# A delta-rule attention with two feed-forward layers on one core: k loaded by tokens and turned on TensorE, v scaled before the triangular solve, weights issued earlier, weight conversion dealt out in pairs

## The chip, the cores and the metric

One core of a Trainium2 chip runs the whole program. The metric is device time in microseconds (us) of one launch, the median of repeated runs. PE is TensorE, DVE is VectorE, ACT is ScalarE, POOL is GpSimd, SP is SyncE; SP, ACT and POOL can also issue DMA transfers, each from a queue of its own, in order.

## The reference, cut to what matters

```
# attention: B=4, H=8, S=768, D=48
k_n = k / (norm(k) + 1e-6); state = zeros(B, H, D, D)
for t in range(S):
    y[:, :, t] = q[:, :, t] @ state
    v_old = state^T k_n[:, :, t]
    state += beta[:, :, t] * outer(k_n[:, :, t], v[:, :, t] - v_old)
# first layer: 3072 tokens, 384 -> 2048 -> 384
x = (s * relu(y @ w_in)**2 + b) @ w_out
# second layer: 8 experts, 384 -> 1024 -> 384, the best expert of each token by cosine / tau
out = gate * (relu(x @ w1[e]) @ w2[e])
```

## The kernel before

The sequence of 768 tokens is cut into chunks of C = 32 tokens, and four chunks (HG = 4, 128 tokens) make a group; there are NG = 6 groups. For each group the kernel prepares and then runs the attention.

- Preparation: `load_k`, `load_q`, `load_v`, `load_beta` issue the loads. k lies in `kpad` with 32 tokens by four pairs of heads on the partitions, one slot per chunk s. `tr_k` and `tr_q` turn k and q on PE into `kqt` (features on partitions), `gram` (for group 0 `gram_first`) multiplies k with k and with q, `lanes_in` transposes the products on DVE into `A` and normalises, and a triangular solve follows on DVE: `solve`, or for groups 0 and 1 `solve_d` on the two halves of the triangle, 15 steps of two instructions, after which `off_in` transposes twice (`tt`, `dd`) and `off_1`, `off_2` put the missing quarter together with 64 small matmuls each per chunk. `scale_v`, inside `lanes_in`, multiplies v by the norms of k on POOL.
- Attention of a group, `dstep` for s = 0 to 3, each three hops: `ks` (PE: state times k and q; DVE: `X`), `tx` (PE: `u`; DVE: `bdu`), then `ku` (PE: `ds`; DVE: the state `sst`) and `mu` (PE: the output into `ch`; ACT copies it to `x`). Each waits for the one before. `ku` reads k in the layout with 32 tokens by four pairs (`kpad`).

The first layer (`moe1`) runs on PE in ticks between the hops: `mm1` and `mm2` over eight pairs of weight blocks for each of 12 tiles of 256 tokens. Its products are fp32r with operands split into a high and a low part, so the weights are first converted: they lie interleaved in 16 units, and `convert()` takes each apart with two ACT operations (`w_scale`), two DVE operations, one POOL addition (L577), one ACT copy and one subtraction (L562, on POOL, or on DVE for every second unit from the sixth on). `w_step()` advances `convert()` by half a unit.

PE, DVE, ACT and POOL run in the order in which the code is written; SP's loads stand in the order in which the tile framework places them. For group 0 nothing of the first layer can run, since it needs the attention's output. For group 0 the items of the list in `attention` are keyed by hop; those with keys of 100 and more, the preparation of group 1, come after group 0's attention, with ticks of the first layer between them (`PREP`: 2 ticks after each turn, 12 after `lanes_in`, 3 after each solve step, 10 after `off_in`, 1 after each `off_`). From group 1 on, the preparation of the next group runs between the hops of this one, and `run_moe` is dealt out so that the first layer stays one group behind.

```
elif st["gi"] == 0:
    if nh % 4 == 1:
        w_step()              # one half unit per hop of group 0's attention
...
if state["n"] % 4 == 0:
    w_step()                  # and one per four ticks of the first layer
```

Of the kernel before, what the change touches and what calls it, by code (L numbers as in the profile page):

```python
# [19 lines left out]
def tile_kernel(ctx, tc, q, k, v, beta, w_in, w_out, s_in, b_in, emb, tau, w1, w2, out):  # L20
# [103 lines left out]

    def load_v(gi, eng, heads=range(B)):
# [8 lines left out]

    def load_q(gi, engines):
        i = 0
        for h in range(B):
            for g in range(2):
                engines[i % len(engines)].dma_start(
                    out=qpad[:, h, :, 64 * g:64 * g + D],  # L140
                    in_=q[h, g::2, gi * HG * C:(gi + 1) * HG * C, :].rearrange("r t d -> t r d"))
                i += 1
# [22 lines left out]
    def tr_q(gi, h, alt=False):  # L165
        pp = ps_pp.tile([128, 4, HG, C], F32, tag="pp", name="pp")
        for r in range(4):
            nc.tensor.transpose(out=pp[0:DP, r].rearrange("p n t -> p (n t)"), in_=qpad[:, h, r, 0:DP], identity=ident)
        for s in range(HG):
            o = kqt_t[gi, s][:, h].rearrange("p (a x t) -> p a x t", a=2, x=4)[:, :, 1:3, :]  # L170
            i = pp[0:DP, :, s, :].rearrange("p (a x) t -> p a x t", a=2)
            nc.scalar.copy(out=o, in_=i)
# [49 lines left out]
    ln = {}  # L222

    def lanes_in(gi):
        if gi < 2:
            Af = stg.tile([128, C + 1, C], F32, tag="A", name="A")
            Tf = stg.tile([128, C + 1, C], F32, tag="gc", name="T")
# [6 lines left out]
        nc.gpsimd.memset(Tf, 0.0)  # L234
# [27 lines left out]
        if gi > 1:  # L262
            scale_v()
        return scale_v
# [33 lines left out]
    def tail_solve(gi, scale_v):  # L298
        scale_v()
        off_in(gi)  # L300

# [8 lines left out]
    def off_1(gi, n0, n1):  # L310
# [8 lines left out]
        zz = stg.tile([128, 2 * B, n1 - n0, C2], F32, tag="tmp", name="zz")  # L319
# [109 lines left out]
    def dstep(gi, s, more):  # L429
# [6 lines left out]
        if nb:  # L436
            X = ks(gi, s, ch)
            if gi == 0:
                warm(3)
            yield  # L440
        bdu = tx(gi, s, X)
        if gi == 0:
            warm(0 if s == 0 else 2 if s == 1 else 3)
# [9 lines left out]
    def attention(more, first):  # L453
        for gi in range(NG):
# [5 lines left out]
            if gi == 0:  # L460
                add(0, first)
                for n0, n1, h in ((1, 2, 0.0), (2, 4, 2.0)):
                    add(h, off_1, 0, n0, n1)
                    add(h + 1.0, off_2, 0, n0, n1)
            if gi + 1 < NG:
                g2 = gi + 1
                sy = [nc.sync]
                if gi:
                    add(0, load_k, g2, sy)
                    add(0, load_q, g2, sy)  # L470
                    add(0, load_beta, g2)
                    add(0, load_v, g2, nc.sync)
                h = 3.25 if gi else 100
                dh = 0.25 if gi else 1
                for f in (tr_k, tr_q, gram):
                    for s in range(0, HG, 2 if f is gram else 1):
                        if gi == 1 and f is tr_k and s == 3:
                            h = max(h, 6.25)
                        add(h, f, g2, s)
                        h += dh  # L480
# [8 lines left out]
                else:  # L489
                    add(103.5, router_setup_a2)  # L490
                    add(104.5, router_setup_b)
                    lv = []
                    add(200, lambda: lv.append(lanes_in(1)))
                    for j in range(C2 - 1):
                        add(300 + j, solve_d, 1, j)
                    add(400, lambda: tail_solve(1, lv[0]))
# [19 lines left out]
            while items:  # L516
                t = items[0][0]
                due(t)
                yield PREP.get(t // 100, 2)
# [36 lines left out]
    def w_parts(n):  # L556
# [4 lines left out]
        eng = nc.gpsimd if n % 2 or n < 5 else nc.vector  # L561
        eng.tensor_tensor(out=w[:, :, 1], in0=x, in1=w[:, :, 0].bitcast(F32), op=ALU.subtract)  # L562
# [20 lines left out]
    def w_step():  # L583
        next(cg_, None)

# [212 lines left out]
    with tc.manual_schedule(engines={ET.PE, ET.DVE, ET.Activation, ET.Pool}):  # L798
        hw, sy = [nc.sync, nc.scalar], [nc.sync]
        setup()  # L800
        sq0 = stg.tile([128, 1], F32, tag="ss", name="sq0")
        nc.vector.memset(sq0, 1.0)
        nc.scalar.activation(out=sq0, in_=sq0, func=AF.Sqrt)
        load_k(0, hw)
        warm_t.append(ps_h.tile([128, 2, 256], F32, tag="h", name="warm"))
        load_beta(0, nc.gpsimd)
        w_load(W_ORDER[0])
        load_v(0, nc.sync, (0,))
        load_q(0, sy)
        for i in range(1, B):  # L810
# [398 lines left out]
```

## Time and profile before

| | |
|---|---|
| median of three runs | 1013.82 us (1010.84 to 1013.82) |
| the profiled execution | 1013.74 us, span 1011.7 us |
| mean granted PE clock | 0.914 |
| PE busy, matmul instructions | 876.2 us (87%), 13070 |
| DVE, ACT, POOL busy | 468.4, 321.8, 287.0 us |

```
PE   2587963996599799979997999999998999999997
DVE  1744698135942794269525962225314323321111
POOL 4124666113032333243323332334530110110100
PEclk9657876797599899999999999999998999999999
GB/s 111 221 56 278 34 29 66 5 34 27 49 25 34 3 50 32 49 3 45 37 18 3 18 2 18 2 17 128 46 17 49 42 38 41 47 50 162 16 32 24
```

Each digit is the busy share of a fortieth of the span (25.3 us) in tenths; PEclk is the granted clock in tenths of 2.4 GHz; GB/s is what the DMA engines moved. The first eleven digits of PE are the start, group 0, the preparation of group 1 and group 1; the rest is the first layer with groups 2 to 5, and from about 760 us the second layer.

### The profile page before, as it was taken

What the parts mean: (1) busy time and instruction counts of PE and PEld (TensorE: products, weight loads), DVE (VectorE), ACT (ScalarE), POOL (GpSimd) and SP (SyncE); (2) the same over time, 40 slices, a digit from 0 to 9 for tenths busy, and PEclk for the clock granted to TensorE, in tenths of its full rate; (3) what the DMA queues carried; (4) which work ended last, traced back from release to release, by engine and by line L of the source; (5) the groups of instructions that cost most, each with busy time, mean ns of one, the idle gap of its engine ahead of it and who ended that gap; (6) DMA issues with size and microseconds to landing.
All of it is one profiled execution on the core that took longest, in us unless ns stands there. A gap on an engine that the chain in (4) does not pass through costs nothing. (4 is left out here: it accounts for less than half of the span.)

```text
span 1011.7 us, 29675 instructions
## 1 busy us (share of the span) xinstructions
PE 876.2 (87%) x13070; PEld 803.7 (79%) x13070; DVE 468.4 (46%) x975; ACT 321.8 (32%) x674; POOL 287.0 (28%) x289
## 2 busy tenths in 40 slices
PE   2587963996599799979997999999998999999997
PEld 2374863885499799979897989999996779779896
DVE  1744698135942794269525962225314323321111
ACT  1235643142134233413341333335422222222221
POOL 4124666113032333243323332334530110110100
PEclk9657876797599899999999999999998999999999
DMA  5738213011211021202200000004103811114000
GB/s 111 221 56 278 34 29 66 5 34 27 49 25 34 3 50 32 49 3 45 37 18 3 18 2 18 2 17 128 46 17 49 42 38 41 47 50 162 16 32 24
DMA packets 115986, 49.55 MB, mean 49 GB/s; under 512 B 90328, under 2 KB 112529, under 8 KB 115857
## 3 DMA queue, kind: packets, MB, share of 16 engines
q1 hardware_dynamic: 112976, 47.23, 20.4%
q8 instruction: 103, 1.69, 0.7%
q10 hardware_dynamic: 2304, 0.39, 0.3%
q14 instruction: 27, 0.21, 0.1%
q0 software_dynamic: 576, 0.02, 0.0%
HBM read 38.06 MB, written 9.74 MB: 47 GB/s over the span
## 5 line engine op out<-in xcount | busy, mean ns | idle before, releaser
L641 PE MATMUL h<-xhl,wp 128*128 128x256 f32 x1728 | 254.0, 297 | 44.0 <-ACT r L649 30.2
L641 PEld LDWEIGHTS h<-xhl,wp 128*128 128x128 f32 x1728 | 226.1, 200 | 50.7 <-ACT r L649 33.0
L650 POOL TENSOR_TENSOR r<-r 128x512 f32<-128x512 f32 x96 | 104.6, 1090 | 352.9 <-ACT r L649 352.7
L673 PE MATMUL acc<-gh,wp 128*128 128x256 f32 x1152 | 161.5, 286 | 0.0
L673 PEld LDWEIGHTS acc<-gh,wp 128*128 128x128 f32 x1152 | 146.3, 193 | 4.4 <-issue 2.6
L653 DVE TENSOR_TENSOR gl<-r,gh 128x512 fp32r<-128x512 f32 x96 | 73.8, 769 | 129.7 <-ACT gh L652 129.5
L652 ACT CAST gh<-r 128x512 fp32r<-128x512 f32 x96 | 59.8, 622 | 149.6 <-POOL r L651 149.2
L919 DVE SCALAR_TENSOR_TENSOR hl<-h,hh 128x512 fp32r<-128x512 f32 x46 | 31.7, 691 | 141.2 <-ACT hh L918 141.2
L649 ACT ACTIVATE r<-h 128x512 f32<-128x512 f32 x96 | 57.4, 598 | 109.9 <-PE h L641 89.4
L651 POOL TENSOR_SCALAR r<-r,s_sb,b_sb 128x512 f32<-128x512 f32 x96 | 82.2, 856 | 10.0
L673 PE MATMUL acc<-gl,wp 128*128 128x256 f32 x576 | 83.9, 281 | 0.0
L673 PEld LDWEIGHTS acc<-gl,wp 128*128 128x128 f32 x576 | 74.4, 191 | 0.2
L416 ACT COPY x<-ch 32x384 f32<-32x384 f32 x96 | 45.1, 470 | 73.5 <-PE ch L402 72.5
L988 POOL TENSOR_TENSOR x2l<-xr,x2h 128x512 fp32r<-128x512 f32 x15 | 18.7, 1276 | 166.2 <-ACT x2h L987 166.2
L999 PE MATMUL o<-w2h,hh 128*128 128x384 f32 x184 | 62.3, 339 | 0.0
L999 PE MATMUL o<-w2l,hh 128*128 128x384 f32 x184 | 61.9, 336 | 0.0
L999 PE MATMUL o<-w2h,hl 128*128 128x384 f32 x184 | 61.8, 336 | 0.0
L273 DVE TENSOR_TENSOR T<-T,tmp 128x31 f32<-128x31 f32 (+15 forms) x124 | 55.2, 445 | 4.3
L916 PE MATMUL h<-x2l,w1h 128*128 128x512 f32 x120 | 51.8, 431 | 4.6 <-POOL x2l L988 4.6
L916 PE MATMUL h<-x2h,w1h 128*128 128x512 f32 x120 | 50.4, 420 | 6.1 <-ACT x2h L987 4.9
L270 DVE TENSOR_TENSOR tmp<-A,T 128x31 f32<-128x31 f32 (+15 forms) x124 | 53.5, 431 | 3.0
L918 ACT ACTIVATE hh<-h 128x512 fp32r<-128x512 f32 x46 | 27.4, 598 | 85.4 <-PE h L916 85.4
(207 smaller groups left out, 1227.6 us busy)
## 6 DMA issues: line engine op xcount, KB each, us to landing
wr<-in_moe_w_in SPq DMA_DIRECT2D x16, 384.0 KB
wr<-in_moe_w_out SPq DMA_DIRECT2D x8, 768.0 KB
v<-in_v SPq DMA_DIRECT2D x192, 24.0 KB
qpad<-in_q SPq DMA_DIRECT2D x48, 96.0 KB
x2d<-x2s SPq DMA_DIRECT2D x24, 192.0 KB
out<-o SPq DMA_DIRECT2D x24, 192.0 KB
kpad<-in_k SPq DMA_DIRECT2D x176, 24.0 KB
xr<-x2d SPq DMA_DIRECT2D x5, 768.0 KB
```

The costliest lines, as they stand in the source:

```text
L270: nc.vector.tensor_tensor(out=tmp, in0=A[:, j + 1:, j:j + 1].to_broadcast([128, m, j + 1]), in1=T[:, j:j + 1, 0:j + 1].to_broadcast([128, ...
L273: nc.vector.tensor_tensor(out=T[:, j + 1:, 0:j + 1], in0=T[:, j + 1:, 0:j + 1], in1=tmp, op=ALU.subtract)
L416: nc.scalar.copy(out=x_t[gi][pb:pb + C, :, r * 96:(r + 1) * 96].rearrange("p h (g e) -> p h g e", g=2), in_=y[32 * rr:32 * rr + 32, :, :, ...
L641: nc.tensor.matmul(out=h[:, f, :], lhsT=wi_(w, 2 * j + f, m), rhs=x[:, m, :], start=(m == 0 and i == 0), stop=(m == KD - 1 and i == 2))
L649: nc.scalar.activation(out=r, in_=h, func=AF.Relu)
L650: nc.gpsimd.tensor_tensor(out=t, in0=r, in1=r, op=ALU.mult)
L651: nc.gpsimd.tensor_scalar(out=t, in0=t, scalar1=s_sb, scalar2=b_sb, op0=ALU.mult, op1=ALU.add)
L652: later.append((step[0] + 7, lambda: nc.scalar.copy(out=gh, in_=t)))
L653: later.append((step[0] + 9, lambda: nc.vector.tensor_tensor(out=gl, in0=t, in1=gh.bitcast(F32), op=ALU.subtract)))
L673: nc.tensor.matmul(out=acc[:, m * TT:(m + 1) * TT], lhsT=wo_(w, 2 * j + f, m * 128, 128), rhs=x[:, f, :], start=(j == 0 and m not in seen ...
L916: nc.tensor.matmul(out=ps, lhsT=w[:, m, f * 128:(f + 1) * 128], rhs=x[:, m, :], start=(m == 0 and i == 0), stop=(m == KD - 1 and i == 2))
L999: nc.tensor.matmul(out=ps, lhsT=h[:, sl], rhs=w[:, f, :], start=(f == 0 and i == 0), stop=(f == KF2 - 1 and i == 2))
```

## The change

- k of groups 0 and 1, and every q, come with `load_n`: 128 tokens on the partitions, one transfer for a head pair's four rows, 8 transfers for a group in place of 32. Group 0's k is split over SP's and ACT's queues, its q stands on ACT's queue. `tr_n` turns k and q alike. The other layout of k, which `ku` needs, is made for group 0 by `k_rows` on PE (16 matmuls and one ACT copy per chunk), and for group 1 by a second load.
- `scale_v` runs in `lanes_in`, ahead of the solve, for all groups.
- For group 0 three of four `off_1` stand ahead of the attention, one `off_2` per hop follows; 22 warm-up matmuls stand at the start, 12 instead of 9 in the solve, fewer between the hops.
- Weights 8 to 15 are issued on SP ahead of group 1's q, beta and v.
- Conversion in group 0's attention comes in pairs of half units (`convert_piece`), and in the first layer one half unit per five ticks instead of four; every L562 is on POOL.

```diff
+    def load_n(gi, t, src, eng, heads=range(B)):
+        for h in heads:
+            for g in range(2):
+                eng.dma_start(
+                    out=t[:, h, :, 64 * g:64 * g + D],
+                    in_=src[h, g::2, gi * HG * C:(gi + 1) * HG * C, :].rearrange("r t d -> t r d"))
...
+    def tr_n(gi, h, t, x, engines):
...
+            if engines[s % len(engines)] is nc.scalar:
+                nc.scalar.copy(out=o, in_=i)
+            else:
+                nc.vector.tensor_copy(out=o, in_=i)
+
+    def tr_kn(gi, h):
+        tr_n(gi, h, kpad[gi], slice(0, 4, 3), (nc.scalar, nc.vector))
+    def k_rows(gi, s):
+        pp = ps_pp.tile([128, B, DP], F32, tag="pp", name="kr")
+        for h in range(B):
+            for r in range(4):
+                c = r // 2 * 128 + r % 2 * 96
+                nc.tensor.matmul(out=pp[32 * r:32 * r + 32, h, :], lhsT=kqt_t[gi, s][:, h, c:c + 32],
+                                 rhs=ident[0:DP, 0:DP], start=True, stop=True)
+        nc.scalar.copy(out=kpad[gi][:, :, s, :], in_=pp)
...
-        if gi > 1:
-            scale_v()
-        return scale_v
+        scale_v()
...
             if gi == 0:
+                add(0, off_2, 0, 1, 2)
                 add(0, first)
-                for n0, n1, h in ((1, 2, 0.0), (2, 4, 2.0)):
-                    add(h, off_1, 0, n0, n1)
-                    add(h + 1.0, off_2, 0, n0, n1)
+                add(0.1, k_rows, 0, 1)
+                add(1, off_2, 0, 2, 3)
+                add(1.1, convert_piece)
+                add(2, off_2, 0, 3, 4)
+                add(2.1, k_rows, 0, 2)
+                add(4.1, k_rows, 0, 3)
+                for i in range(3, 3 * HG - 2):
+                    if i % 3 != 2:
+                        add(i, convert_piece)
+                add(10, convert_piece)
...
+                    for i in range(B):
+                        add(99 if i < 2 else 100, tr_kn, 1, i)
+                    add(100, load_k, 1, [nc.sync])
...
-        eng = nc.gpsimd if n % 2 or n < 5 else nc.vector
-        eng.tensor_tensor(out=w[:, :, 1], in0=x, in1=w[:, :, 0].bitcast(F32), op=ALU.subtract)
+        nc.gpsimd.tensor_tensor(out=w[:, :, 1], in0=x, in1=w[:, :, 0].bitcast(F32), op=ALU.subtract)
...
+    def convert_piece():
+        w_step()
+        w_step()
...
+        load_n(0, kpad[0], k, nc.sync, range(0, B, 2))
+        load_n(0, kpad[0], k, nc.scalar, range(1, B, 2))
...
-        load_k(0, hw)
+        load_n(0, qpad, q, nc.scalar)
...
+        warm(22)
+        for i in range(B):
             load_v(0, nc.sync, (i,))
             w_load(W_ORDER[i])
...
-        w_scale(2)
-        scale_v()
         off_in(0)
-        off_1(0, 0, 1)
-        w_step()
+        for n in range(3):
+            off_1(0, n, n + 1)
+        convert_piece()
         off_2(0, 0, 1)
-        w_step()
-        warm(3)
+        off_1(0, 3, 4)
...
-                if state["n"] % 4 == 0:
+                if state["n"] % 5 == 0:
                     w_step()
```

Three places show what moves. First SP's queue from the start of the program (a row is one line's consecutive transfers with the shape of one; `wr` is a raw weight unit). Before:

```order
L120 DMA kpad_103<-in_k 32x4x48 x16
L536 DMA wr_183<-in_moe_w_in 128x3x256 x2
L131 DMA v<-in_v 32x4x48 x8
L139 DMA qpad<-in_q 128x4x48 x8
L536 DMA wr_203<-in_moe_w_in 128x3x256 x2
L131 DMA v<-in_v 32x4x48 x8
L536 DMA wr_214<-in_moe_w_in 128x3x256 x2
L131 DMA v<-in_v 32x4x48 x8
L540 DMA wr_225<-in_moe_w_out 128x2x768
L131 DMA v<-in_v 32x4x48 x8
```

And of the change:

```order
L128 DMA kpad_103<-in_k 128x4x48 x4
L138 DMA v<-in_v 32x4x48 x8
L570 DMA wr_200<-in_moe_w_in 128x3x256 x2
L138 DMA v<-in_v 32x4x48 x8
L570 DMA wr_211<-in_moe_w_in 128x3x256 x2
L138 DMA v<-in_v 32x4x48 x8
L570 DMA wr_222<-in_moe_w_in 128x3x256 x2
L138 DMA v<-in_v 32x4x48 x8
```

Sixteen small transfers of k have become four large ones, q has left this queue for ACT's, and all of v stands nearer to the front.

Second DVE around the solve of group 0 (`nmc` is the transposed norm that `scale_v` waits for, `tmp` and `T` are the solve). Before, its end:

```order
L290 TENSOR_TENSOR tmp<-A,T 128x30
L293 TENSOR_TENSOR T<-T,tmp 128x2x15
L256 STREAM_TRANSPOSE nmc<-nm 128x32
L305 STREAM_TRANSPOSE tt<-T 128x32x32
L307 STREAM_TRANSPOSE dd<-T 128x32x32
```

And of the change, its beginning:

```order
L270 COPY T<-bt 128x32
L271 TENSOR_TENSOR A<-A,bt 128x1024
L277 STREAM_TRANSPOSE nmc<-nm 128x32
L309 TENSOR_TENSOR tmp<-A,T 128x30
L312 TENSOR_TENSOR T<-T,tmp 128x2x15
```

What releases POOL's two multiplications of v has moved from behind the solve to ahead of it.

Third PE in the second step of group 0's attention, from `tx` (u) to `ku` (ds). Before:

```order
L317 MATMUL z_1064<-tt,gc 32x16 x64
L367 MATMUL u<-X,tt 32x48 x32
L424 LDWEIGHTS ident
L424 MATMUL warm<-ident 128x512
L424 LDWEIGHTS ident
L424 MATMUL warm<-ident 128x512
L330 MATMUL z_1172<-zz,dd 32x16 x64
L383 MATMUL ds<-bdu,kpad_103 64x96
```

And of the change:

```order
L351 MATMUL z_1184<-zz,dd 32x16 x32
L189 MATMUL kr<-ident,kqt 32x112 x16
L388 MATMUL u<-X,tt 32x48 x32
L445 LDWEIGHTS ident
L445 MATMUL warm<-ident 128x512
L445 LDWEIGHTS ident
L445 MATMUL warm<-ident 128x512
L404 MATMUL ds<-bdu,kpad_103 64x96
```

The 128 matmuls of `off_2` for two chunks no longer stand between u and ds; ahead of u one chunk's `off_2` and one `k_rows` stand in place of 128 matmuls of `off_1`.

## Rows read from the trace of the kernel before

**Rows 1.** Stretches: busy us and instructions by engine, granted clock, DMA share, GB/s.

```profile
129.00:168.00 39.00, 21.42 (x136) 20.33 (x134) 37.10 (x52) 15.88 (x22) 24.98 (x18) 0.78 0.31 54
168.00:194.00 26.00, 17.54 (x557) 15.28 (x557) 7.59 (x11) 4.38 (x10) 9.51 (x8) 0.63 0.09 16
...
282.00:760.00 478.00, 454.85 (x7406) 439.29 (x7394) 244.14 (x495) 170.63 (x373) 166.95 (x171) 0.99 0.12 29
```

**Rows 2.** Timeline, start and length in us: loads, k's transposes, v's scaling, warm-up.

```profile
0.81 8.89 SPq L120 DMA_DIRECT2D kpad<-in_k  x16
...
16.66 3.00 PE L157 MATMUL pp<-ident,kpad 128*112 128x128 f32 x13 [4.41 <-DMA v<-in_v]
...
19.70 0.69 DVE L161 COPY kqt<-pp 112x512 f32<-112x512 f32 x1 [1.02 <-PE pp L157]
...
28.78 1.50 SPq L536 DMA_DIRECT2D wr<-in_moe_w_in  x2
...
36.03 4.80 SPq L131 DMA_DIRECT2D v<-in_v  x8
...
37.97 3.81 PE L424 MATMUL warm<-ident 128*128 128x512 bf16 x9
...
42.64 2.91 POOL L260 TENSOR_TENSOR v<-v,nmc 128x768 f32<-128x768 f32 x2 [29.32 <-DMA v<-in_v]
```

**Rows 3.** Timeline, DVE: last gram copy, first and last solve step, the second transposition.

```profile
25.68 0.42 DVE L830 COPY gc<-gr 128x256 f32<-128x256 f32 x1 [3.67 <-ACT gc L832]
...
32.30 0.21 DVE L290 TENSOR_TENSOR tmp<-A,T 128x30 f32<-128x30 f32 x1
...
40.75 0.19 DVE L293 TENSOR_TENSOR T<-T,tmp 128x30 f32<-128x30 f32 x1
...
42.75 1.99 DVE L307 STREAM_TRANSPOSE dd<-T 128x1024 f32<-128x1024 f32 x1
```

**Rows 4.** Stretches of 10 us, columns as in group 1.

```profile
0.00:10.00 10.00, 0.87 (x2) 0.34 (x2) 0.98 (x5) 1.49 (x2) 8.82 (x31) 1.00 0.44 65
...
80.00:90.00 10.00, 5.95 (x196) 4.19 (x199) 5.23 (x8) 5.59 (x9) 6.67 (x5) 0.79 1.02 324
```

**Rows 5.** Timeline, PE, DVE, ACT: group 0's attention, the first product of the layer.

```profile
47.26 1.01 PE L367 MATMUL u<-v,tt 32*32 32x48 f32 x37
...
51.30 0.77 PE L367 MATMUL u<-v,tt 32*32 32x48 f32 x26 [3.03 <-issue]
...
52.20 1.02 DVE L372 TENSOR_TENSOR bdu<-u,par 128x384 f32<-128x384 f32 x2 [5.10 <-PE u L367]
...
66.76 1.91 PE L330 MATMUL z<-zz,dd 32*32 32x16 f32 x128 [0.29 <-issue]
...
70.76 2.25 PE L383 MATMUL ds<-bdu,kpad 64*64 64x96 f32 x32 [2.10 <-DVE wr L576]
...
87.56 0.46 PE L346 MATMUL ch<-sst,kqt 48*64 48x48 f32 x7 [3.96 <-issue]
...
94.78 1.93 ACT L416 COPY x<-ch 32x384 f32<-32x384 f32 x4 [5.36 <-PE ch L402]
...
99.82 2.11 PE L641 MATMUL h<-xhl,wp 128*128 128x256 f32 x6 [2.40 <-ACT xhl L606]
...
194.06 1.96 PE L346 MATMUL ch<-sst,kqt 48*64 48x48 f32 x64
```

**Rows 6.** Timeline, POOL scaling v while DVE solves, group 2.

```profile
246.18 2.91 POOL L260 TENSOR_TENSOR v<-v,nmc 128x768 f32<-128x768 f32 x2 [4.04 <-DVE nmc L256]
...
247.73 1.42 DVE L273 TENSOR_TENSOR T<-T,tmp 128x31 f32<-128x31 f32 x1
```

**Rows 7.** Groups by line, 129 to 168 us: busy us, mean ns of one.

```profile
L577 POOL TENSOR_TENSOR wa<-wr 128x768 int32<-128x768 int32 x7 | 11.3, 1620 | 18.7 <-issue 12.0 <-DVE wr L576 6.7
...
L562 POOL TENSOR_TENSOR wp<-wa,wp 128x768 fp32r<-128x768 f32 x3 | 5.6, 1864 | 0.9 <-ACT wp L560 0.9
...
L562 DVE TENSOR_TENSOR wp<-wa,wp 128x768 fp32r<-128x768 f32 x4 | 3.8, 948 | 0.0
```

More of the change, by code (lines that the diff above doesn't have):

```diff
@@ L222, in tile_kernel @@
     ln = {}
+    T0 = []
     def lanes_in(gi):
@@ L437, in dstep @@
             X = ks(gi, s, ch)
-            if gi == 0:
-                warm(3)
+            if gi == 0 and s > 1:
+                warm(2)
             yield
         bdu = tx(gi, s, X)
-        if gi == 0:
-            warm(0 if s == 0 else 2 if s == 1 else 3)
+        if gi == 0 and s:
+            warm(2)
         yield
@@ L469, in attention @@
                     add(0, load_k, g2, sy)
-                    add(0, load_q, g2, sy)
+                    add(0, load_n, g2, qpad, q, nc.sync)
                     add(0, load_beta, g2)
                     add(0, load_v, g2, nc.sync)
[L473 to L480, printed above, removed]
+                h = 3.25
+                if gi:
+                    for f in (tr_k, tr_q, gram):
+                        for s in range(0, HG, 2 if f is gram else 1):
+                            add(h, f, g2, s)
+                            h += 0.25
+                else:
+                    for i in range(B):
+                        add(99 if i < 2 else 100, tr_kn, 1, i)
+                    add(100, load_k, 1, [nc.sync])
+                    for f in (tr_q, gram):
+                        for s in range(0, HG, 2 if f is gram else 1):
+                            add(100, f, 1, s)
                 if gi:
@@ L833, in tile_kernel @@
         wa = xh_ring([128, 2, 2 * DM], I32, "wa")
-        scale_v = lanes_in(0)
+        lanes_in(0)
         cg = ps_c.tile([128, 2, HG * B, C], F32, tag="ch", name="gr")
-        w_scale(1)
         for h in range(B):
             tr_q(0, h)
-        load_q(1, sy)
-        for i in W_ORDER[8:]:
-            w_load(i)
+        load_n(1, qpad, q, nc.sync)
         load_beta(1)
         load_v(1, nc.sync)
+        router_setup_a()
+        k_rows(0, 0)
+        w_scale(2)
         for s in range(HG):
@@ L847, in tile_kernel @@
             solve_d(0, j)
-            if j == 9:
+            if j == 7:
                 tg = ln[0][1]
-                nc.tensor.matmul(out=warm_t[0][0:32, 0, 0:32], lhsT=tg[:, 8, 0:32], rhs=tg[:, 9, 0:32],
+                nc.tensor.matmul(out=warm_t[0][0:32, 0, 0:32], lhsT=tg[:, 6, 0:32], rhs=tg[:, 7, 0:32],
                                  start=True, stop=True)
-                warm(9)
-        w_scale(2)
-        scale_v()
+                warm(12)
         off_in(0)
-        off_1(0, 0, 1)
-        w_step()
+        for n in range(3):
+            off_1(0, n, n + 1)
+        convert_piece()
         off_2(0, 0, 1)
-        w_step()
-        warm(3)
+        off_1(0, 3, 4)
         def masks():
```

80 lines of the change are left out of this document (37 added, 43 removed).

## The prediction

> **What bounds the kernel now.** I read the stretches first, to find where PE is not the bound, then the timeline of those places, then the groups by line there.
>
> From 282 to 760 us PE is busy 454.85 of 478 us at a granted clock of 0.99 [rows 1]. There PE is the bound, and the change takes no work off it there. So what it gains or loses lies ahead of that, and a gain there moves all the rest. The mark I go by is the first matmul of group 1's attention, 194.06 us [rows 5]. Three stages lead to it.
>
> Stage 1, to the first u at 47.26 [rows 5], is a chain. SP needs 8.89 us to issue its 16 transfers of k, and PE turns the last thirteen blocks only from 16.66, after 4.41 us of waiting [rows 2]. The last copy of turned k ends at 20.39 (19.70 + 0.69) [rows 2], the last copy of the gram products at 26.10, the solve runs from 32.30 to 40.94, the second transposition ends at 44.74 [rows 3].
>
> Stage 2, group 0's attention, ends with the copies of x at 96.71, and the first layer starts at 99.82 [rows 5]. PE, DVE and PE again wait for each other. Beside that PE shows three gaps: 3.03 us inside the first u, 2.10 ahead of the second ds, 3.96 inside the last product with the state; two of them carry "issue", so nothing that the profile shows released them [rows 5].
>
> Stage 3, the preparation of group 1, has its core from 129 to 168 us: DVE busy 37.10 of 39 us, POOL 24.98, PE 21.42 [rows 1]. DVE's time is partly waiting for POOL: a solve instruction that takes 0.19 us alone [rows 3] took 1.42 us while POOL scaled v [rows 6].
>
> **The change part by part.** The profiled execution took 1013.74 us, 2.0 more than its span and 0.1 from the median of the runs, so the sum stands for both.
>
> 1. *k by tokens.* SP issued one transfer per 0.56 us (8.89 / 16) [rows 2]. Four on each of two queues are out after 2.2 us, at 3.0. The data are the same: 32 blocks of 32 x 4 x 48 values of 4 bytes, 786 KB. The first 10 us moved 65 GB/s at a share of 0.44 [rows 4], so 148 GB/s when full, and 786 KB take 5.3 us. k lands no earlier than 8.3 (3.0 + 5.3), and no later than 10.0 if the lag of before stays, from the last issue at 9.70 to 16.66 [rows 2]. The 22 warm-ups, at 0.42 each (3.81 / 9) [rows 2], last 9.3 us and end near 10.8 if they begin at 1.5 (an estimate), earlier if the clock rises. Sixteen transposes at 0.23 (3.00 / 13) [rows 2]: at best only the last four stand behind the landing, and k is turned by 9.6 with a copy; at worst all sixteen stand behind the warm-ups, 10.8 + 3.7 + 0.7 = 15.2. I take 12.5, about the middle: **-7.9** against 20.39 (ends -10.8 and -5.2). gram, norms and solve keep their lengths, so the solve would run from 24.4 to 33.0.
>
> 2. *v scaled ahead of the solve.* SP's order gives k 2.2, four times v at 4.80 and three weight units at 1.50 [rows 2], so the last v is issued at 26.7; with the lag of before (40.83 to 42.64 [rows 2]) it lands at 28.5, in the middle of the solve. POOL's two multiplications last 2.91 us; DVE gets through about one instruction beside each of them [rows 6]: **+2.4** (0 if they fall behind the solve, 2.9 if DVE gets through none). The Trainium skill, page SBUF — State Buffer, section "Who interferes with whom", says that a DVE instruction with two inputs in SBUF and a GpSimd instruction that reads SBUF shut each other out for the whole instruction, whichever starts first; the trace agrees (1.42 us instead of 0.19 [rows 6]), and by the rule alone the term would be 2.9 and the sum 0.5 higher.
>
> 3. *Group 0's attention.* The second ds no longer stands behind 128 `off_2` matmuls, 1.91 us, and the gap behind them, 2.10 [rows 5]: -4.0 (-1.9 if the gap stays). `k_rows` is not in the trace. Its nearest row are the 32 ds matmuls of 96 columns in 2.25 us [rows 5], 0.070 each; sixteen of 112 columns make 1.3 us. Below, half of that if PE runs at 2.4 GHz (the slices above show a clock of 0.5 for this time); above, 0.23 each as for the transposes [rows 2], 3.7. The first stands with 64 `off_2` matmuls (half of 1.91 [rows 5]) beside bdu, 1.02 us [rows 5]: 0.96 + 1.3 - 1.02 = +1.2. The second, again with 64, replaces 128 matmuls of `off_1`, of the size of `off_2`'s: +0.35. The third stands bare ahead of the next product with the state: +1.3. Together +2.9 (ends +0.9 and +10). The conversion pairs on DVE cost nothing where each lies beside a ds of 2.25 us [rows 5]; uncovered, one POOL subtraction of 1.86 us [rows 7] would hold up each. Fewer warm-ups are hidden by bdu as before. The gaps of 3.03 and 3.96 stay, I assume. Net **-1.1**.
>
> 4. *Start of the first layer.* From the last x copy to the first product 3.1 us pass (96.71 to 99.82 [rows 5]), on ACT. Now six small copies and one more conversion cast stand there in place of one large copy; I take half as much again: **+1.5** (0 to 3.1).
>
> 5. *Preparation of group 1.* By the code 16 half units have been dealt out when it begins, before 14; and by the end of the solve, 79 ticks on, 15 of the remaining 18 at one per five ticks, where before all 20 had been. That is five half units, 2.5 units, less ahead of the solve's end. A unit on POOL is 1.62 + 1.86 = 3.5 us [rows 7], and DVE waits for POOL or works: -8.7. What is put behind falls where POOL is busy 9.51 of 26 us [rows 1], at nothing. Five subtractions go from DVE, 0.95 each, to POOL, 1.86 each [rows 7]: +4.6 where the two exclude each other. v's scaling goes from beside the transposes into the solve: +2.4 as in 2. Net **-1.7** (-13.4 if DVE alone sets the pace, since then the five also save 4.7; +3.5 if POOL alone does: -8.7 + 9.3 + 2.9).
>
> The later loads cost nothing: group 1's second load of k is needed 95 us after the first layer begins (99.82 to 194.06 [rows 5]), and 32 issues at 0.56 are 18 us. The loads of weights stand ahead of those of q, beta and v for group 1, which is not needed before stage 3.
>
> Sum: -7.9 + 2.4 - 1.1 + 1.5 - 1.7 = -6.8, so 1013.74 - 6.8 = 1006.9, **1007 us**.
>
> **The rivals.**
>
> *A. The gaps go too.* The gap of 3.96 lies where the DMA engines are full, 324 GB/s at a share of 1.02 [rows 4], with the second half of the weights. With these issued by about 50 us, both "issue" gaps may vanish: another -7.0, 1000 us. For it speaks that place; against it that the weights now crowd around 25 to 50 us, where `off_1`, `off_2` and the first u come.
>
> *B. The gain is used up.* POOL sets the pace in stage 3: its queue there gets five subtractions and v's scaling, and term 5 is +3.5 instead of -1.7: -7.9 + 2.4 - 1.1 + 1.5 + 3.5 = -1.6, 1012 us. For it speaks POOL's 24.98 us beside DVE's 37.10 in 39 [rows 1], 62 in all; against it that POOL itself is idle 14 us there. Or that crowd of weights gives two more gaps, of 3.03 and 3.96: 1006.9 + 7.0 = 1014. It decides from 4 us on.
>
> *C. Slower: weights late for PE.* Before, conversion ran ahead of use. At one half unit per five ticks the lead shrinks: the consumer k of sixteen comes at tick 6k and needs 2k + 4 half units, while 16 + 1.2k have been dealt out; at k = 10 that is four ahead, at k = 13 less than two. If PE waits at each of the last four for POOL's addition and subtraction, 3.5 us each [rows 7], that is +14: 1021 us. It decides from 10 us on (three of the four). Against it speaks that PE idles 17.6 of 39 us there anyway [rows 1], so that the lead in time is longer than in ticks.
>
> **How the numbers follow.** A change of 0.3%, 3 us, is about what a measurement here can tell from none. The forecast, 1000 to 1011 about 1007, has a chance of 0.46; A, 994 to 1002, 0.20; B, 1011 to 1016, 0.19; C, above, 0.15. Faster: forecast and A, and the little of B below 1010.8, 0.67; same 0.18; slower 0.15. The range leaves out the lower half of A and most of C: 997 to 1016. The likeliest case's own range, 1000 to 1011, stands beside it.
>
> **What would show it.** The last copy of turned k near 12.5 instead of 20.39, the solve's first instruction near 24.4 and a solve longer than 8.6 us with two instructions above 1 us in it (terms 1, 2); the second ds right behind bdu, and `kr` of 1.3 us (term 3); the first product near 94.7 (99.82 - 7.9 + 2.4 - 1.1 + 1.5), 129 to 168's successor with less DVE time (term 5), group 1's attention near 187, and from there to the end the same length. Wrong it would be if stage 3 lasts longer than 94 us (B, C: PE waiting for POOL L595), if `kr` takes over 3 us, or if the part from group 1's attention on changes by itself.

## The result and the profile after

| | |
|---|---|
| before, median of 5 runs | 1013.82 us (1010.84 to 1014.57) |
| after, median of 5 runs | 1020.56 us (1018.81 to 1022.22) |
| ratio after to before | 1.0069, 95% interval 1.0049 to 1.0089 |
| the profiled execution of after | 1018.81 us, span 1017.1 us, mean granted clock 0.917 |

The change made the kernel slower by 0.7%, above the range of 997 to 1016. The profiled execution is the fastest of the five, so the table accounts for 5.1 of the 6.7 us between the medians. The marks, in us from the span's start (before by [rows 2, 3, 5]; the forecasts 39.2 and 90.1 follow from the prediction's terms):

| mark | before | forecast | after | after - before |
|---|---|---|---|---|
| last copy of turned k ends | 20.39 | 12.5 | 14.76 | -5.6 |
| first solve starts | 32.30 | 24.4 | 26.54 | -5.8 |
| second transposition (dd) ends | 44.74 | 39.2 | 41.31 | -3.4 |
| group 0's first u starts | 47.26 | | 51.78 | +4.5 |
| last copy of x ends | 96.71 | 90.1 | 102.47 | +5.8 |
| first product of the layer | 99.82 | 94.7 | 109.81 | +10.0 |
| group 1's first product with the state | 194.06 | 187 | 207.45 | +13.4 |
| the execution | 1013.74 | 1007 | 1018.81 | +5.1 |

The gain at the start is real. It is more than lost between dd and the first product, a little more goes in the preparation of group 1, and then, where the prediction expected nothing, some 8 us come back (13.4 to 5.1).

The timeline of ACT, DVE and POOL in the changed kernel, first 42 us (before: [rows 2, 3]; L174 and L176 copy turned k, L281 scales v, L309 and L312 are the solve, L322 the second transposition):

```profile
8.05 2.99 ACTq L128 DMA_DIRECT2D qpad<-in_q  x4
11.08 0.27 ACT L174 COPY kqt<-pp 112x128 f32<-112x128 f32 x1 [6.52 <-DMA qpad<-in_q]
11.38 0.29 DVE L176 COPY kqt<-pp 112x128 f32<-112x128 f32 x1 [8.70 <-ACT kqt L174]
...
14.47 0.29 DVE L176 COPY kqt<-pp 112x128 f32<-112x128 f32 x1 [0.33 <-ACT kqt L174]
...
26.54 0.19 DVE L309 TENSOR_TENSOR tmp<-A,T 128x30 f32<-128x30 f32 x1
...
32.69 2.94 POOL L281 TENSOR_TENSOR v<-v,nmc 128x768 f32<-128x768 f32 x2 [19.18 <-DMA v<-in_v]
32.81 1.48 DVE L312 TENSOR_TENSOR T<-T,tmp 128x110 f32<-128x110 f32 x1
34.32 1.41 DVE L309 TENSOR_TENSOR tmp<-A,T 128x96 f32<-128x96 f32 x1
...
39.34 1.97 DVE L322 STREAM_TRANSPOSE dd<-T 128x1024 f32<-128x1024 f32 x1
```

ACT's first copy comes only when its queue has issued q (8.05 + 2.99 = 11.04), and from there each copy waits for the one on the other engine. While POOL scales v, two solve instructions take 1.48 and 1.41 us.

TensorE in the changed kernel, 39 to 110 us, with ACT's last copies of x (before: [rows 5]; L437 copies x, L332 off_1, L351 off_2, L388 u, L404 ds, L367 the product with the state, L169 turning k, L640 transposing x, L678 the first layer):

```profile
39.63 1.78 PE L332 MATMUL z<-tt,gc 32*32 32x16 f32 x117 [0.66 <-DVE tt L320]
46.04 1.19 PE L332 MATMUL z<-tt,gc 32*32 32x16 f32 x74 [4.63 <-issue]
47.04 0.21 PE L351 MATMUL z<-zz,dd 32*32 32x16 f32 x2
47.08 0.21 PE L332 MATMUL z<-tt,gc 32*32 32x16 f32 x1
47.08 0.86 PE L351 MATMUL z<-zz,dd 32*32 32x16 f32 x50
50.73 0.34 PE L351 MATMUL z<-zz,dd 32*32 32x16 f32 x11 [2.80 <-issue]
...
54.58 0.45 PE L388 MATMUL u<-v,tt 32*32 32x48 f32 x11 [1.51 <-issue]
...
60.89 1.44 PE L404 MATMUL ds<-bdu,kpad 64*48 64x96 f32 x14 [1.83 <-issue]
...
67.36 0.41 PE L351 MATMUL z<-zz,dd 32*32 32x16 f32 x14 [3.01 <-issue]
67.70 1.96 PE L367 MATMUL ch<-sst,kqt 48*64 48x48 f32 x64
69.58 0.92 PE L351 MATMUL z<-zz,dd 32*32 32x16 f32 x50
73.83 0.40 PE L351 MATMUL z<-zz,dd 32*32 32x16 f32 x14 [3.32 <-issue]
...
78.00 1.71 PE L404 MATMUL ds<-bdu,kpad 64*64 64x96 f32 x32
...
100.56 1.91 ACT L437 COPY x<-ch 32x384 f32<-32x384 f32 x4
107.55 1.69 PE L640 MATMUL xp<-ident,x 128*128 128x128 f32 x6 [5.82 <-DVE kqt L176]
109.81 2.03 PE L678 MATMUL h<-xhl,wp 128*128 128x256 f32 x6 [0.57 <-ACT xhl L643]
```

Six gaps marked "issue", 17.1 us in all, where the kernel before had four between 47 and 97 us of 8.2 in all (the two large ones in [rows 5]). Count the matmuls from one to the next: 74 + 2 + 1 + 50 = 127 to the second, 14 + 64 + 50 = 128 to the last. The third part of the profile page has one line that fits such a step:

```profile
q8 instruction: 104, 1.70, 0.7%
```

104 packets of 1.70 MB are 16.3 KB each, and TensorE's 13213 matmuls with as many weight loads make 26426 instructions, 254 for each packet if the queue is TensorE's: 127 matmuls with their loads. So I read the gaps as TensorE waiting for its next packet of instructions. The trace's record of queue q8 bears this out: each of the six gaps ends 1.2 to 1.6 us after one packet of 16384 bytes has landed (that of 43.42 to 44.49 for the gap that ends at 46.04, that of 71.10 to 72.42 for the last), and so do the four of the kernel before (that of 48.75 to 49.84 for the one that ends at 51.30). The DMA engines were full for most of this; only the last gap falls where they are not (columns as in [rows 4]):

```profile
40.00:50.00 10.00, 3.31 (x231) 3.10 (x224) 2.67 (x3) 0.80 (x3) 1.46 (x1) 0.50 1.04 321
50.00:60.00 10.00, 6.82 (x254) 5.97 (x254) 3.51 (x9) 0.80 (x2) 0.00 (x0) 0.50 0.95 277
60.00:70.00 10.00, 6.10 (x238) 5.61 (x241) 2.71 (x4) 4.15 (x7) 1.92 (x1) 0.50 1.05 381
70.00:80.00 10.00, 6.52 (x210) 5.07 (x206) 4.97 (x8) 2.83 (x4) 3.31 (x3) 0.63 0.47 95
```

Under that load the packets start 6.2 to 6.4 us apart (52.23, 58.44, 64.85, 71.10), and TensorE is through with one in 1.9 to 4.5 us. In the kernel before, at shares of 0.42 and 0.28 (50 to 70 us), they start 3.7 to 4.0 us apart (56.34, 60.15, 64.18, 67.88), and the gaps there are 0.97 and 0.29 us. A full DMA is not needed for a gap, though: behind 181 matmuls of gram in 2.37 us the kernel before stands 2.56 us, until 36.45, at a share of 0.27.

The preparation of group 1 in three stretches (the first product, the solve of group 1, up to its attention), and the part that [rows 1] gave for 282 to 760 us:

```profile
109.81:144.97 35.16, 28.13 (x423) 26.13 (x423) 22.47 (x43) 17.45 (x42) 17.15 (x14) 0.88 0.23 38
144.97:182.47 37.50, 17.00 (x114) 16.07 (x114) 36.22 (x44) 13.93 (x20) 31.77 (x21) 0.83 0.29 51
182.47:207.45 24.98, 16.15 (x552) 13.83 (x552) 7.49 (x10) 3.77 (x9) 5.09 (x4) 0.64 0.01 3
282.00:760.00 478.00, 456.13 (x7497) 440.06 (x7497) 248.69 (x507) 171.71 (x374) 166.01 (x169) 0.99 0.14 31
```

From the first product to group 1's attention it is 97.6 us, 94.2 before (99.82 to 194.06 [rows 5]). In the last of the three TensorE does little at first:

```profile
176.19 0.82 PE L640 MATMUL xp<-ident,x 128*128 128x128 f32 x6
...
182.50 1.91 DVE L320 STREAM_TRANSPOSE tt<-T 128x1024 f32<-128x1024 f32 x1
184.27 1.90 DVE L322 STREAM_TRANSPOSE dd<-T 128x1024 f32<-128x1024 f32 x1
186.00 0.57 DVE L609 TENSOR_SCALAR wr<-wr 128x768 int32<-128x768 int32 x1
186.64 1.47 POOL L610 TENSOR_TENSOR wa<-wr 128x768 int32<-128x768 int32 x1 [4.45 <-DVE wr L609]
188.14 0.83 ACT L594 CAST wp<-wa 128x768 fp32r<-128x768 f32 x1 [7.75 <-POOL wa L610]
188.88 0.85 ACT L643 CAST xhl<-xp 128x384 fp32r<-128x384 f32 x2
...
189.79 3.94 PE L678 MATMUL h<-xhl,wp 128*128 128x256 f32 x15 [12.78 <-ACT xhl L643]
```

TensorE has transposed the next x by 177.0 and waits 12.78 us for its copies (L643) on ACT. They stand behind a conversion cast (L594), this waits for POOL's addition (L610), this for DVE's shift (L609), and the shift stands in DVE's queue behind the solve and both transpositions.

### The profile page after: what moved, and what is told of

Same layout as the page of the kernel before. It is cut to its first block, busy times and chain, and to the rows that moved or that the text cites. A ratio compares the mean times of both kernels' runs of the same rounds, so it can differ in the third digit from the quotient of the medians.

```text
span 1017.1 us, 29943 instructions
## 1 busy us (share of the span) xinstructions
PE 875.7 (86%) x13213; PEld 801.1 (79%) x13213; DVE 484.9 (48%) x984; ACT 324.7 (32%) x689; POOL 301.8 (30%) x294
## 5 line engine op out<-in xcount | busy, mean ns | idle before, releaser
L678 PE MATMUL h<-xhl,wp 128*128 128x256 f32 x1728 | 250.9, 295 | 43.4 <-ACT r L686 29.8
L678 PEld LDWEIGHTS h<-xhl,wp 128*128 128x128 f32 x1728 | 224.0, 199 | 50.4 <-ACT r L686 32.6
L437 ACT COPY x<-ch 32x384 f32<-32x384 f32 x96 | 45.2, 471 | 69.7 <-PE ch L423 68.7
L949 PE MATMUL h<-x2l,w1h 128*128 128x512 f32 x120 | 49.6, 414 | 6.5 <-POOL x2l L1021 6.5
```

The source lines that it names most:

```text
L437: nc.scalar.copy(out=x_t[gi][pb:pb + C, :, r * 96:(r + 1) * 96].rearrange("p h (g e) -> p h g e", g=2), in_=y[32 * rr:32 * rr + 32, :, :, ...
L678: nc.tensor.matmul(out=h[:, f, :], lhsT=wi_(w, 2 * j + f, m), rhs=x[:, m, :], start=(m == 0 and i == 0), stop=(m == KD - 1 and i == 2))
L949: nc.tensor.matmul(out=ps, lhsT=w[:, m, f * 128:(f + 1) * 128], rhs=x[:, m, :], start=(m == 0 and i == 0), stop=(m == KD - 1 and i == 2))
```

## The experiments

Ratios are to the kernel before on the same chip, with 95% intervals; after itself stands at 1.0069. Single executions of one kernel lie up to 6.6 us from their median, so the ratios decide, and a profile only says where. Edits are to the changed kernel unless the text says "before"; line numbers of profiles shift a little with them.

Two theories stood against each other at first. T1: the later weights, issued ahead of waiting loads, crowd the DMA engines while TensorE runs its many small matmuls. T2: the conversion's new pace and POOL's subtractions hold the end of group 0's attention and stage 3.

**The crowd of transfers.** First the later weights moved back alone, then the reverse, in the kernel before.

```diff
         load_n(1, kpad[1], k, nc.sync)
-        for i in W_ORDER[8:]:
-            w_load(i)
...
         load_beta(1)
+        for i in W_ORDER[8:]:
+            w_load(i)
         load_v(1, nc.sync)
```

> The changed kernel with one thing moved back: the second half of the weights is issued behind group 1's q and beta, not ahead of them. In the changed kernel TensorE shows six gaps marked issue between 40 and 74 us, 17.1 us in all, while the DMA engines are full (shares 1.04, 0.95, 1.05), and from the second on they stand exactly 127 or 128 matmuls apart. Theory T1 (the crowd of transfers delays something that TensorE needs once per 128 matmuls): the last four gaps (9.7 us in all, 54 to 74) shrink by at least half, the first product comes at about 104 instead of 109.8, and the time falls by about 5, to 1015. Theory T2 (paired conversion pieces and POOL's subtractions hold the second half of group 0's attention and stage 3): the gaps may go, but VectorE and POOL set the end of group 0's attention anyway; 1019 to 1021.

Measured: 1.0043 (1.0023 to 1.0063), 1017.1 us. The first product came at 105.98. Two gaps (5.08 and 2.52) stayed ahead of 51 us, where units 4 to 7 land, and one of 2.05 at 53 to 55 us, where the DMA share had fallen to 0.33; the last three shrank to one of 0.58, and two of 2.1 and 2.0 came at 72 and 78 us with the moved units (DMA share 1.04 from 70 to 80 us). This is T1's direction at about half its size (0.26%, 0.5% forecast), and the interval overlaps that of the change, so the gain in time is not clear of noise.

```diff
# before
+        for i in W_ORDER[8:]:
+            w_load(i)
         load_k(1, sy)
...
         load_q(1, sy)
-        for i in W_ORDER[8:]:
-            w_load(i)
```

> The kernel before with one thing of the change: the second half of the weights is issued ahead of group 1's k (from about 44.5 us) instead of behind its q (from 79 us). T1 (full DMA engines delay something that TensorE needs once per 128 matmuls): the gap of 3.96 us at 87 goes, two to four gaps of 1.5 to 3.5 us appear between 45 and 65 us, and the first product comes 1 to 6 us later than at 99.8; the time is 1014 to 1020. Rival (the gaps come from the order of the matmuls in the changed kernel, not from the transfers): the gap at 87 goes and none takes its place, 1010.

Measured: 1.0051 (1.0029 to 1.0074). The gap of 3.96 at 87 us [rows 5] is gone, and four stand in 48 to 69 us, with the DMA share at 0.92 to 1.06 from 40 to 60 us. TensorE's timeline there:

```profile
49.78 0.77 PE L367 MATMUL u<-v,tt 32*32 32x48 f32 x26 [2.03 <-issue]
...
56.25 1.25 PE L402 MATMUL ch<-bdu,mt 32*32 32x48 f32 x51 [1.99 <-issue]
...
62.72 1.94 PE L346 MATMUL ch<-sst,kqt 48*64 48x48 f32 x59 [3.89 <-issue]
...
68.91 0.99 PE L317 MATMUL z<-tt,gc 32*32 32x16 f32 x59 [1.79 <-issue]
...
89.09 0.33 PE L346 MATMUL ch<-sst,kqt 48*64 48x48 f32 x7 [0.43 <-issue]
...
102.43 2.11 PE L641 MATMUL h<-xhl,wp 128*128 128x256 f32 x6 [2.41 <-ACT xhl L606]
```

The first product is 2.6 us later than in the kernel before, and the order of its matmuls is untouched. So the transfers decide where the long gaps fall. The sum of the gaps from 47 to 97 us went from 8.2 only to 10.1.

**The conversion.** The whole of it undone, then its halves, then the halves of the half that mattered.

```diff
-                add(1.1, convert_piece)
...
+            elif st["gi"] == 0:
+                if nh % 4 == 1:
+                    w_step()
...
-                if state["n"] % 5 == 0:
+                if state["n"] % 4 == 0:
...
-        nc.gpsimd.tensor_tensor(
+        eng = nc.gpsimd if n % 2 or n < 5 else nc.vector
+        eng.tensor_tensor(
```

> The changed kernel with the whole conversion paced as before: one half unit per step in group 0's attention instead of pairs, one per four ticks in the layer instead of five, the later subtractions alternating between POOL and VectorE instead of all on POOL. T2 (pairs and POOL's subtractions cost the second half of group 0's attention and stage 3): the first product comes 4 to 6 us earlier than at 109.8, the time is about 1014. T1 (the crowd of transfers is the cause): the gaps of 40 to 74 stay, the first product moves by less than 2 us, the time stays within 2 us of 1020.6.

Measured: 0.9991 (0.9969 to 1.0013). The first product came at 106.57, 3.2 earlier (4 to 6 forecast). The gaps from 41 to 75 us stayed (17.5 us in all), so each theory holds a part.

The pairs alone back (the first two pieces of that diff):

> The changed kernel with only the pairing of conversion pieces in group 0's attention undone: one half unit at every step as before; the layer's pace of five ticks and all subtractions on POOL stay. The three parts together gave 7 us. If the pairs are the cost (the stretch from the second ds at 78.0 to the first product at 109.8, where sst and X stand behind VectorE's conversion operations of 1.7 to 2.1 us): 1014 to 1016, the first product at 106 to 107. If stage 3's POOL is the cost: 1019 to 1021.

Measured: 1.0141 (1.0097 to 1.0185), slower than the change. The first product did come early, 106.08, but group 1's attention late, 213.77. Who waits for POOL's subtraction (L590 there), between 140 and 215 us:

```profile
  PE acc L705: 10.8, 4
  PE h L673: 5.0, 2
```

Fourteen half units instead of sixteen were dealt out by the first product, and at one per five ticks TensorE ran into the units that were not ready: 15.8 us, where rival C had 14.

The layer's part alone back (the last two pieces):

> The changed kernel with only the layer's part of the conversion undone: one half unit per four ticks, the later subtractions alternating between POOL and VectorE; the pairs stay. If rival B's POOL (five more subtractions of 1.8 to 2.0 us in stage 3) is the cost: group 1's preparation, 109.8 to the end of its solve at 182.5, falls from 72.7 us to about 68 and the time to 1015 to 1016. If the pairs are the cost: 1019 to 1021.

Measured: 1.0014 (0.9990 to 1.0037). Group 1's solve ended at 181.73, hardly earlier, but its attention began at 199.1 instead of 207.45.

> The changed kernel with only the layer's pace of conversion undone: one half unit per four ticks instead of five; all subtractions stay on POOL. Undoing pace and subtractions together gave 0.55%, and there the wait of TensorE at 177 to 190 us for the next tile of x (12.8 us, its copies standing on ACT behind a conversion cast that waits for POOL) was gone. Theory Q (the pace leaves one conversion piece over, which then stands in ACT's and VectorE's queues between the end of group 1's solve and the next tile): the wait goes here too, ratio 1.001 to 1.003. Rival (POOL's five more subtractions are what is late): the wait stays, 1.006 to 1.008.

Measured: 1.0002 (0.9982 to 1.0021). That is just below theory Q's range. One digit, the 5, is worth 0.67%. Its three stretches, as above for the change:

```profile
108.32:144.15 35.83, 29.19 (x423) 27.25 (x423) 24.75 (x44) 17.55 (x42) 19.96 (x15) 0.84 0.24 42
144.15:182.14 37.99, 19.03 (x129) 18.23 (x129) 36.71 (x45) 15.65 (x23) 32.27 (x22) 0.82 0.25 46
182.14:199.49 17.35, 15.32 (x536) 13.20 (x536) 5.67 (x7) 2.18 (x6) 1.81 (x2) 0.56 0.02 4
```

The last is 17.4 us instead of 25.0, and TensorE's wait for the copies of x is gone: the cast of that unit was through at 176, ahead of the solve's end.

> The changed kernel with only the later subtractions alternating between POOL and VectorE again, the pace of five ticks kept. Theory Q: the wait at 177 to 190 us stays, group 1's solve ends 2 to 4 us earlier, ratio 1.004 to 1.007. Rival (POOL's subtractions): the wait goes, 1.001 to 1.003.

Measured: 1.0055 (1.0035 to 1.0075); the wait stayed (12.1 us) and group 1's solve ended 1.3 us earlier (2 to 4 forecast). So it is the pace and not POOL's share of the work: theory Q holds.

**v scaled behind the solve** (groups 0 and 1):

```diff
-        scale_v()
+        if gi > 1:
+            scale_v()
+        return scale_v
...
+        scale_v()
         off_in(0)
```

> The changed kernel with v scaled behind the solve again for groups 0 and 1. By the prediction's term 2 this is worth -2.4 at the end of the first solve and as much in group 1's: two solve instructions of 1.48 and 1.41 us fall to 0.2 each. If these stand on the path all the way: 1016. Rival: the end of the solve is not the path, since TensorE's next gap (4.63 us at 41.4 to 46.0) is not released by the solve, and v is then needed by the first u behind POOL's 3 us: 1019 to 1022.

Measured: 1.0026 (1.0002 to 1.0050), whose upper edge only just touches the change's interval. dd ended at 39.29, 2.0 earlier, yet the first u started at 51.95: the gaps ate it. Group 1's solve took 35.2 us instead of 37.5. Its profiled execution was its slowest (1019.35), so where the gain arises is not shown.

**The preparation of group 2.** The rule that the change drops, put back, and dropped in the kernel before:

```diff
                         for s in range(0, HG, 2 if f is gram else 1):
+                            if gi == 1 and f is tr_k and s == 3:
+                                h = max(h, 6.25)
                             add(h, f, g2, s)
```

> The changed kernel with the fourth transposition of group 2's k, and with it all of group 2's preparation, held back to step 6.25 as in the kernel before. Between the third product with the state of group 1 and the first of group 2 the changed kernel takes 42.1 us (241.4 to 283.4), the kernel before 52.1 (220.7 to 272.9). Theory P (the dropped rule, which the prediction gave no price, starts group 2's solve earlier beside group 1's attention and gains the 8 to 10 us by which the changed kernel catches up there): 1028 to 1031. Rival: the catch-up comes from elsewhere (work of the layer already done, the clock): within 2 us of 1020.6.

Measured: 1.0141 (1.0104 to 1.0178), 1026.4 us. From the third product with the state of group 1 to the first of group 2 it took 51.1 us (237.16 to 288.30) instead of 42.1. Most of that is shifted, not added: the third product itself comes 26.3 us behind the first here and 33.9 in the change, and from group 1's first product to group 2's it is 77.4 us instead of 76.0.

> The kernel before with one thing of the change: the rule that holds the fourth transposition of group 2's k, and what follows it, to step 6.25 is dropped. Theory P (this alone is worth the 7 us that putting the rule back into the changed kernel cost): about 1006. Rival (in the kernel before the wait moves to another place, since its stage 3 ends earlier): 1011 to 1014.

Measured: 0.9952 (0.9929 to 0.9975), 1006.9 us; the same stretch 42.2 us (228.34 to 270.55), and from group 1's first product to group 2's 76.4 us instead of 78.8. Theory P holds in both directions: 0.5 to 0.7% from two lines. From group 1's first product to the end the profiles show 4.4 us more with e4 than in the change (815.8 and 811.4) and 3.8 less with b2 than before (815.8 and 819.7).

**Two small edits that missed.** `add(100, tr_kn, 1, i)` for all heads, and q by `nc.gpsimd`, behind beta on that queue:

> The changed kernel with only one head of group 1's k turned ahead of the first layer's transpositions of x, as the code before had one step there, instead of three. Between the last copy of x and the first product the changed kernel takes 7.3 us (102.47 to 109.81), the kernel before 3.1. Theory of term 4 (the small copies of turned k, six by the prediction, with ACT and VectorE waiting for each other, stand in that way): the stretch falls to about 4.5 us and the time by 2 to 3, to 1018. Rival (the conversion pieces and POOL hold that stretch): 1020 to 1021.

Measured: 1.0119 (1.0086 to 1.0153). The stretch fell from 7.3 to 5.4 us, and group 1's solve began at 149.87 instead of 144.97, since each head now waits for a turn of the layer: slower by 5 us.

> The changed kernel with group 0's q issued by POOL's queue instead of ACT's. In the changed kernel ACT issues q until 11.04 us, and only then come its copies of turned k, though TensorE had turned the first from 8.31 on; the last copy ends at 14.76, 2.3 behind the forecast of 12.5. Expected: k turned by 12 to 13 and the first solve 2 us earlier. If the gaps from 41 us on belong to the transfers, as T1 says, the end does not gain more than 1 us (1019.6 to 1021); if the chain of the first solve sets the time, 1018.5.

Measured: 1.0078 (1.0052 to 1.0104). The first solve began 1.8 us earlier (24.73), but q landed late, since POOL first issues beta (until 12.35 us) and then q from 13.13 to 24.71: TensorE waited 3.87 and 3.45 us for it at 19 to 28 us with gram and u queued behind, and the first u came at 57.02. The run does not tell what an earlier k alone is worth. The Trainium skill, page DMA: Bandwidth & Descriptors, section "Issuing engines are not separate DMA queues", says that transfers issued by different engines run on the same 16 DMA engines and that another issuer saves issue time alone; the 1.8 us agree; the late q comes from its place behind beta, on which the page's sentence says nothing.

**Put together.** The three parts undone at once (e1's, e2's and e3's edits):

> The changed kernel with three of its parts undone together: the later weights issued behind q and beta of group 1, the conversion paced as before, v scaled behind the solves. What is left of the change is k by tokens with its rows made on TensorE, the order of the off_ products, and the earlier preparation of group 2. If the three gains measured alone (-3.5, -7.0, -4.3 against 1020.6) add up: 1006. If conversion and transfers share one path, as T1 and T2 both claim the end of group 0's attention: 1009 to 1010.

Measured: 0.9986 (0.9961 to 1.0011). The single gains (0.26, 0.78 and 0.43%) would make 0.9922: they do not add up. The two gaps ahead of 50 us stayed, 5.51 and 3.89, and the first u at 50.83.

On top of these three, the weights go between the transfers of single heads:

```diff
-        for i in W_ORDER[4:8]:
-            w_load(i)
-        load_n(1, kpad[1], k, nc.sync)
-        for i in W_ORDER[8:]:
-            w_load(i)
+        for i in range(B):
+            w_load(W_ORDER[4 + i])
+            load_n(1, kpad[1], k, nc.sync, (i,))
...
-        load_n(1, qpad, q, nc.sync)
+        for i in range(B):
+            load_n(1, qpad, q, nc.sync, (i,))
+            w_load(W_ORDER[8 + i])
         load_beta(1)
-        load_v(1, nc.sync)
+        for i in range(B):
+            w_load(W_ORDER[12 + i])
+            load_v(1, nc.sync, (i,))
```

> As the run with three parts undone, but the later weights are not issued in a block: each of the last twelve units is issued between the transfers of one head of group 1's k, q or v, so that the DMA engines are never full for long. T1 predicts that the gaps between 40 and 90 us (14 us in all with the weights behind q and beta) shrink to under 8 us, and the time is 3 to 6 us below that of the run with the three parts undone. If instead the gaps depend on the transfers of k and q themselves, or on the number of matmuls alone: no difference.

Measured: 0.9945 (0.9915 to 0.9975). The gaps from 38 to 100 us still add up to 16.9 us (16.8 with the three parts undone), one of 2.90 among them at a share of 0.42 (84.96 to 87.86); by that mark T1's number is missed. The time fell as it said, but the two intervals overlap.

Then units 4 to 7 ahead of the last head of v (`if i == B - 1: ... w_load(j)` in the loop over v):

> As the run with the spread weights, but units 4 to 7 of the weights are issued ahead of the last head of v, so that they land while VectorE solves (25 to 38 us) and TensorE has little to do, and not at 40 to 50 us, where the products off_1, off_2 and the first u show two gaps of 3.6 and 3.4 us (DMA share 1.12). T1: these two shrink by 4 us or more together, the first u comes at 46 to 47 instead of 50.4, and the ratio to the kernel before falls from 0.9945 to about 0.990. Rival (the gaps belong to the many small matmuls themselves): they stay, 0.9945.

Measured: 0.9901 (0.9877 to 0.9926).

> The run with the weights under the solve once more, unchanged, beside the three above on one chip, for a profile of it and a narrower interval: 0.990 of the kernel before again, 0.987 to 0.993.

Measured: 0.9924 (0.9898 to 0.9950), 1002.9 us: this version beats both kernels. TensorE's gaps fell only to 13.2 us, one of 4.28 still ahead of the first u, which came at 49.24 (46 to 47 forecast). Another of 3.99 now ends at 37.81, beside the solve, whose second transposition ends no later for it (39.32; 39.36 in the run with the spread weights). Stretches of it (columns as in [rows 4]):

```profile
30.00:40.00 10.00, 4.49 (x133) 2.48 (x134) 9.38 (x23) 0.42 (x1) 0.00 (x0) 0.50 0.82 267
40.00:50.00 10.00, 5.72 (x366) 4.52 (x368) 1.03 (x3) 1.31 (x5) 4.33 (x3) 0.84 0.70 165
60.00:70.00 10.00, 6.67 (x276) 5.96 (x269) 3.22 (x6) 4.36 (x8) 3.29 (x2) 0.50 0.49 145
```

The transfers moved from 40 to 50 us (1.04 in the change, 0.70 here) to 30 to 40 (0.82), where TensorE has little to do.

With e5's and e6's edits added:

> The run before this one with the two edits of one head and of q on POOL's queue added: the sum of what the single runs give, if they act in different places; by the estimates 3 to 5 us below the run with the weights under the solve, about 0.986 of the kernel before.

Measured: 0.9972 (0.9953 to 0.9990): the two edits together cost 0.5 to 0.7% (against 0.9924 and 0.9901), where 0.986 was forecast.

Last, the kernel before with these loads and the earlier preparation, without k by tokens:

> The kernel before, k as before, with the earlier preparation of group 2 (worth 0.48% alone) and with the weights as in the run with them under the solve: units 4 to 7 ahead of the last head of v, the last four between the heads of group 1's v. It asks what k by tokens is worth, since that run (k by tokens, the same loads) stands at 0.990 of the kernel before. If k by tokens still gives its 5 us of an earlier solve when the crowd is out of the way: 0.995 here. If those 5 us are lost again in the attention of group 0 (more and other small matmuls ahead of the first u): 0.990 or lower here.

Measured: 0.9974 (0.9940 to 1.0007). It does not isolate k: behind the four units SP issued the last v only from 39.66 to 51.90 us (36.03 to 40.83 before [rows 2]), so the first u waited for its scaling until 54.61.

## Why the prediction was wrong

**Term 1, k by tokens** (-7.9): -5.6 at the copies, -5.8 at the solve, near the weaker end. q's issues on ACT (1.8 us by e6) and the alternating copies took the rest.

**Term 2, v's scaling** (+2.4): +2.4 at dd (-5.8 to -3.4). The rule of the Trainium skill, page SBUF — State Buffer, section "Who interferes with whom", which has both engines exclude each other for the whole instruction, agrees with the 1.48 and 1.41 us.

**Term 3, group 0's attention** (-1.1): +9.2 from dd to the last copy of x. The second ds did lose its stall (it follows the warm-ups at 78.00 without a gap, in place of 2.10) and `kr` took 0.97 to 1.72 us, near its price of 1.3. That price was lucky: it counted sixteen matmuls by the code at the rate of the trace's rows for ds, and the trace shows two rows for each of these matmuls (`kr` x32), which by that rate make 2.6. Two steps failed. One is "The gaps of 3.03 and 3.96 stay, I assume": I had named the crowd both as a gain (A) and as a loss (B) and counted it at nothing, and it gave 17.1 us of gaps instead of 8.2. The other is an omission: three off_1 moved ahead of the first u, 320 small matmuls there instead of 128, two and a half packets in place of one, while the transfers were at their densest. dd to u takes 10.5 us instead of 2.5, and 7.4 of them are the first two gaps, which stay when the later weights are moved back (e1). No run puts the three off_1 back, so their share is argued, not shown.

**Term 4, the layer's start** (+1.5): +4.2 (7.3 instead of 3.1 us). Conversion pieces and copies share it: with the pieces single it was 5.0 and 5.3 us (e2, f1), with one head's copies 5.4 (e5).

**Term 5, the preparation of group 1** (-1.7): +3.4. The step that failed is "What is put behind falls where POOL is busy 9.51 of 26 us [rows 1], at nothing". An idle POOL does not make it free: the unit put behind stood in the queues of DVE and ACT, ahead of the copies of x for which TensorE waited. Undoing the pace alone turns 97.6 us into 91.2, so the pace is some +6 and the rest of term 5 about -3. Rival C's 1021 is close to the 1020.56 by luck: its wait, TensorE for POOL's L595, is 1.7 us in the change and appears in full only in f1.

**Not priced at all**: the dropped `max(h, 6.25)`. The prediction said that the part from group 1's attention on keeps its length; it became 8.3 us shorter (+13.4 to +5.1). By the profiles of e4 and b2 the rule makes about 4 of them, by their times 5 to 7. Of the 8.3, 2.2 lie behind the last product of the first layer (248.3 us before, 246.1 after), where b1 (246.2), which keeps the rule, is as short; what makes that difference is not shown.

So the sum -5.8 + 2.4 + 9.2 + 4.2 + 3.4 - 8.3 = +5.1 closes. What stays open: what k by tokens alone is worth. With the same early preparation, b2 without it stands at 0.9952 and c3 and f4 with it and better placed loads at 0.990 and 0.992; how much of the difference is k's and how much the loads', no run separates. That the gaps are late instruction packets is shown by the step of 127 or 128 matmuls and by the packet that lands ahead of the end of each; how much of their length is the crowd and how much the many small matmuls is not separated, since they stay at 13 to 17 us in c1, c2 and f4.

## What to carry to other kernels

Where a change moves bulk transfers earlier, look for the stretch with the most small matmuls, not for an idle DMA engine: the transfers belong where TensorE runs few and large instructions. Work "put behind" is priced by what stands after it in every queue that it passes, not by whether its engine is idle. And go through the removed lines of a diff as carefully as the added ones: two of them were worth more than most terms of the sum.

## What was not expected of the hardware

All fifteen stops of TensorE that the timelines of the two kernels mark "issue" between 13 and 90 us end 1.2 to 1.6 us after a packet of queue q8 has landed, one packet for 127 or 128 matmuls with their weight loads. With the DMA engines' share near 1 these stops are 1.5 to 5.4 us long in the change and in e6. Where the share is 0.16 to 0.28 (before 60 to 70, e6 and e4 70 to 80 us) the same steps show 0.3 to 0.9 us, but not everywhere: 2.56 us at 0.27 behind gram in the kernel before.
